# One load of x in place of two, and the second piece of w1 held behind a memset: a gated MLP on one core

## The chip, the cores and the metric

The kernel runs on one core of a Trainium2 chip. The metric is device time in microseconds (us). All times below are of this one core. A run counts as fast or slow by its distance from the fastest run of the same kernel (over 1.5% is slow).

## The reference, cut to what matters

```python
gate = jnp.einsum("bsd,df->bsf", x, w1)     # x: 32 x 32 tokens of 512, w1 and w3: 512 x 1792
up   = jnp.einsum("bsd,df->bsf", x, w3)
out  = jnp.einsum("bsf,fd->bsd", silu(gate) * up, w2)   # w2: 1792 x 512, all bf16
```

There are 1024 tokens. The contraction over 512 is four tiles of 128, called dt 0 to dt 3. The columns of w1 and w3 are 14 tiles of 128.

## The kernel before

Only the start matters here. TensorE runs six matmuls on a constant as its warm-up (0.77 to 3.49 us in the trace), turns the first 256 tokens of x by matmuls against an identity, and then multiplies these 256 tokens with the first four column tiles of w1 and of w3. The weights come in two pieces, dt 0 to 1 and dt 2 to 3. The second 256 tokens come turned by a DMA transpose.

```python
load_x(nc.sync, 0, 1)                                  # 128 tokens, 128 KB, issued by SP
load_x(nc.scalar, 1, 2)                                # 128 tokens, 128 KB, issued by ScalarE
load_w(nc.sync, w1_sb, w1_v, 0, FK, 0, 2)              # w1, dt 0-1, 256 KB
nc.scalar.activation(table[:], one, SIGMOID)           # ScalarE's table load comes here, 1.28 us
load_w(nc.scalar, w1_sb, w1_v, 0, FK, 2, DT)           # w1, dt 2-3, 256 KB
load_w(nc.sync, w3_sb, w3_v, 0, FK, 0, 2)
load_w(nc.sync, w3_sb, w3_v, 0, FK, 2, DT)
nc.sync.dma_start_transpose(out=xT[:, :, HB:NB], in_=x_flat[HB:NB, :])
for c0, c1 in ((FK, 8), (8, FT)):
    load_w(nc.sync, w1_sb, w1_v, c0, c1)
    load_w(nc.sync, w3_sb, w3_v, c0, c1)
# ... cut: one more transpose, w2, warm-up, turning x on TensorE
for dt in range(DT):
    for fo in range(FK):
        project(gates[fo], w1_sb, fo, 0, HB, [dt])     # 16 matmuls of 256 columns, dt by dt
for dt in range(DT):
    for fo in range(FK):
        project(ups[fo], w3_sb, fo, 0, HB, [dt])
```

Of the kernel before, what the change touches and what calls it, by code (L numbers as in the profile page):

```python
# [10 lines left out]
def kernel(  # L11
# [8 lines left out]
    nc = tc.nc  # L20
    P = nc.NUM_PARTITIONS
# [32 lines left out]
    w1_sb = consts.tile([P, DT, F], bf16, name="w1_sb")  # L54
# [6 lines left out]
    def load_x(queue, t0, t1):  # L61
        queue.dma_start(out=x_sb[:, t0:t1, :], in_=x_view[:, t0:t1, :])  # L62

    def load_w(queue, w_sb, w_v, c0, c1, d0=0, d1=DT):
        f0, f1 = c0 * P, c1 * P
        queue.dma_start(out=w_sb[:, d0:d1, f0:f1], in_=w_v[:, d0:d1, f0:f1])
# [1 line left out]
    one = nc.const_aps.tensor(1.0, [P, 1], bf16)  # L68
    table = consts.tile([P, 1], fp32, name="table")

    load_x(nc.sync, 0, 1)
    load_x(nc.scalar, 1, 2)
    load_w(nc.sync, w1_sb, w1_v, 0, FK, 0, 2)
    nc.scalar.activation(table[:], one, SIGMOID)  # L74
    load_w(nc.scalar, w1_sb, w1_v, 0, FK, 2, DT)
# [142 lines left out]
```

## Time and profile before

| kernel before | value |
|---|---|
| median of its six runs beside the changed kernel | 82.45 us (82.25 to 83.01) |
| span of the profiled run | 80.6 us |
| TensorE busy | 75.9 us |
| first gate matmul | 5.07 us |

How to read the profile's lines: the chain of waits lists start, duration and the work that the end hung on; a line of the timeline is start, duration, engine, source line, operation, tile, count, and in brackets how long the engine was idle before and what ended that. SPq and ACTq are the queues on which SP and ScalarE issue transfers.

### The profile page before, as it was taken

Reading aid. Unit: us, or ns where it says so; the run is one execution under the profiler, and the core shown is the slowest. Engines: PE = TensorE matmul, PEld = TensorE weight load, DVE = VectorE, ACT = ScalarE, POOL = GpSimd, SP = SyncE. Lnnn points to the kernel's source line nnn. Section 1 sums busy time; section 2 is a strip of 40 time slices with the busy share of each in tenths; the row PEclk is TensorE's granted clock in tenths of the full one; section 3 lists DMA queues with packets and bytes.
Section 4 is the critical chain, followed back from the end, with each engine's and each line's share of the span. In section 5 each row is a group of like instructions: output and inputs, shape, how many; then the busy total and the mean of one; then the engine's idle time right before and its main releaser. Section 6 shows DMA issues by size and latency. Waiting matters only on the chain.

```text
span 80.6 us, 1063 instructions
## 1 busy us (share of the span) xinstructions
PE 75.9 (94%) x404; PEld 38.8 (48%) x410; DVE 39.4 (49%) x61; ACT 23.2 (29%) x39; POOL 0.7 (1%) x6
## 2 busy tenths in 40 slices
PE   6959999999999999999999999999999999999960
PEld 2348984444444444444444444444444444444850
DVE  0110189999888878878868878872000000000040
ACT  4430274223432223432223432220220220220200
POOL 3000000000000000000000000000000000000000
PEclk9999999999999999999999999999999999999999
DMA  1999999989910000000000000000101102001120
GB/s 24 271 365 273 350 370 370 295 185 355 355 47 0 0 0 0 0 0 0 8 4 0 0 0 0 0 4 0 38 27 65 41 24 73 34 31 65 36 78 17
DMA packets 9893, 7.67 MB, mean 95 GB/s; under 512 B 3744, under 2 KB 9888, under 8 KB 9888
## 3 DMA queue, kind: packets, MB, share of 16 engines
q1 hardware_dynamic: 9472, 7.21, 29.6%
q10 hardware_dynamic: 416, 0.39, 1.4%
q8 instruction: 3, 0.05, 0.3%
q14 instruction: 2, 0.02, 0.1%
HBM read 5.77 MB, written 1.05 MB: 85 GB/s over the span
## 4 chain that ended last, share of the span: by engine, by line
PE 90%; DMA 5%; issue 1%; SPq 0%; DVE 0%; DVEq 0%
PE gate_ps L123 30%; PE o_ps L171 30%; PE up_ps L123 30%; DMA w_sb<-in_w_dram 5%; SPq L62 0%; DVE o_sb L180 0%; DVEq L180 0%
## 5 line engine op out<-in xcount | busy, mean ns | idle before, releaser
L123 PEld LDWEIGHTS <-w_sb 128*128 128x128 bf16 x256 | 25.0, 98 | 24.2 <-DMA w_sb<-in_w_dram 1.1
L123 PE MATMUL gate_ps<-xT,w_sb 128*128 128x512 bf16 (+1 forms) x126 | 28.7, 352 | 1.0 <-DMA w_sb<-in_w_dram 0.9
L123 PE MATMUL up_ps<-xT,w_sb 128*128 128x512 bf16 (+1 forms) x126 | 28.7, 352 | 0.1
L133 ACT ACTIVATE sig<-gate_ps 128x512 f32<-128x512 f32 x28 | 16.7, 597 | 32.0 <-PE gate_ps L123 29.7
L171 PE MATMUL o_ps<-w_sb,hT 128*128 128x512 bf16 (+2 forms) x138 | 24.3, 336 | 0.1
L135 DVE TENSOR_TENSOR t<-gate_ps,sig 128x512 f32<-128x512 f32 x28 | 19.3, 689 | 9.5 <-ACT sig L133 9.5
L136 DVE TENSOR_TENSOR hT<-t,up_ps 128x512 bf16<-128x512 f32 x28 | 19.3, 688 | 3.3 <-PE gate_ps L123 0.5
L171 PEld LDWEIGHTS <-hT 128*128 128x128 bf16 x140 | 12.6, 98 | 12.0
L180 DVE CAST o_sb<-o_ps 128x128 bf16<-128x128 f32 (+1 forms) x3 | 1.0, 336 | 22.3 <-PE o_ps L171 22.3
L182 ACT CAST o_sb<-o_ps 128x512 bf16<-128x512 f32 x7 | 4.1, 586 | 17.9 <-PE o_ps L171 17.9
L94 PE MATMUL warm_ps<-const-bfloat16-1.0 128*128 128x512 bf16 x6 | 2.7, 626 | 0.8 <-PEq L202 0.8
L116 DVE CAST xT<-pT 128x128 bf16<-128x128 f32 (+1 forms) x2 | 0.7, 358 | 3.7 <-PE pT L106 3.7
L94 PEld LDWEIGHTS <-const-bfloat16-1.0 128*128 128x128 bf16 x6 | 0.7, 136 | 1.8 <-issue 1.8
L74 ACT ACT_TABLE_LOAD x1 | 1.3, 1283 | 1.2 <-PEq L202 1.2
L116 ACT CAST xT<-pT 128x128 bf16<-128x128 f32 (+1 forms) x2 | 0.9, 426 | 1.2 <-PE pT L106 1.2
L106 PEld LDWEIGHTS <-x_sb 128*128 128x128 bf16 x8 | 0.5, 101 | 0.9 <-DMA x_sb<-in_x_dram 0.8
L106 PE MATMUL pT<-ident,x_sb 128*128 128x128 bf16 x8 | 0.7, 230 | 0.0
masks.py:199 POOL TENSOR_SCALAR_AFFINE_SELECT ident<-ident 128x128 bf16<-128x128 bf16 x1 | 0.3, 294 | 0.1
masks.py:197 POOL MEMSET ident<- 128x128 bf16 x1 | 0.2, 205 | 0.3 <-POOLq L202 0.3
L74 ACT ACTIVATE table<-const-bfloat16-1.0 128x1 f32<-128x1 bf16 x1 | 0.2, 203 | 0.0
L202 POOL MEMSET const-bfloat16-1.0<- 128x1 bf16 x1 | 0.1, 103 | 0.0
L202 POOL MEMSET const-uint8-127<- 128x1 uint8 x1 | 0.1, 103 | 0.0
(2 smaller groups left out, 0.2 us busy)
## 6 DMA issues: line engine op xcount, KB each, us to landing
w_sb<-in_w_dram SPq DMA_DIRECT2D x2, 896.0 KB, 7.0
w_sb<-in_w_dram SPq DMA_DIRECT2D x2, 768.0 KB, 8.1
w_sb<-in_w_dram SPq DMA_DIRECT2D x2, 512.0 KB, 5.8
out_dram<-o_sb SPq DMA_DIRECT2D x7, 128.0 KB, 1.7
w_sb<-in_w_dram SPq DMA_DIRECT2D x3, 256.0 KB, 4.3
w_sb<-in_w_dram ACTq DMA_DIRECT2D x1, 256.0 KB, 4.0
x_sb<-in_x_dram ACTq DMA_DIRECT2D x1, 128.0 KB, 2.8
x_sb<-in_x_dram SPq DMA_DIRECT2D x1, 128.0 KB, 2.6
```

The lines of the kernel that those rows point to most:

```text
L74: nc.scalar.activation(table[:], one, SIGMOID)
L94: nc.tensor.matmul(warm_ps[:, 0:cols], lhsT=one.to_broadcast([P, P]), rhs=one.to_broadcast([P, cols]), start=True, stop=True,)
L106: nc.tensor.matmul(pT[:, i, j, :], lhsT=x_sb[:, nt, dt * P : (dt + 1) * P], rhs=ident[:], start=True, stop=True,)
L116: copy(xT[:, dts[0] : dts[-1] + 1, nts[0] * P : (nts[-1] + 1) * P], pT[:].rearrange("p d t c -> p d (t c)"),)
L123: nc.tensor.matmul(ps[:, c0 : c0 + n1 - n0], lhsT=w_sb[:, dt, fo * P : (fo + 1) * P], rhs=xT[:, dt, n0:n1], start=(dt == 0), stop=(dt == D ...
L133: nc.scalar.activation(sig[:], gate_ps[:], SIGMOID)
L135: nc.vector.tensor_mul(t[:], gate_ps[:], sig[:])
L136: nc.vector.tensor_mul(hT[:, fo, nb * NB : (nb + 1) * NB], t[:], up_ps[:])
L171: nc.tensor.matmul(o_ps[:], lhsT=hT[:, fo, nt * P : (nt + 1) * P], rhs=w2_sb[:, fo, c0 : c0 + DB], start=(fo == 0), stop=(fo == FT - 1),)
L180: nc.vector.tensor_copy(o_sb[:], o_ps[:])
L182: nc.scalar.copy(o_sb[:], o_ps[:])
L202: nc = _bacc.Bacc("TRN2", target_bir_lowering=False, num_devices=1)
```

## The change

The intent: x goes first, alone and as one load, w1's first piece right behind it on the same queue. ScalarE issues only w1's second piece, and a memset of a part of that piece's place on GpSimd holds it back for a moment, so that it doesn't take bandwidth from x.

```diff
-    load_x(nc.sync, 0, 1)
-    load_x(nc.scalar, 1, 2)
+    nc.gpsimd.memset(w1_sb[:, 2, 0 : 2 * P], 0.0)
+    load_x(nc.sync, 0, 2)
     load_w(nc.sync, w1_sb, w1_v, 0, FK, 0, 2)
     nc.scalar.activation(table[:], one, SIGMOID)
     load_w(nc.scalar, w1_sb, w1_v, 0, FK, 2, DT)
```

## The prediction

> **What bounds the kernel now.** I read four views in turn: the page, the chain that ended last, the start of the timeline, and the transfers split by queue in two stretches of the start.
>
> The page says which engine is the bound, and how little is left beside it.
>
> ```profile
> span 80.6 us, 1063 instructions
> PE 75.9 (94%) x404; PEld 38.8 (48%) x410; DVE 39.4 (49%) x61; ACT 23.2 (29%) x39; POOL 0.7 (1%) x6
> PE 90%; DMA 5%; issue 1%; SPq 0%; DVE 0%; DVEq 0%
> ```
>
> TensorE is busy for 94% of the span. The third line is the chain that ended last: 90% is matmul, and only 5% is a transfer. The chain in order of time tells which transfer.
>
> ```profile
> 0.74 0.39 SPq L62
> 1.13 0.07 issue
> 1.20 3.83 DMA w_sb<-in_w_dram
> 5.02 0.05 issue
> 5.07 1.92 PE gate_ps L123 x16
> 6.99 1.75 PE up_ps L123 x16
> 8.74 0.44 PE gate_ps L123 x4
> ```
>
> So the end is set by the first piece of w1, issued by SP at 1.20 and landed at 5.02 us. The first gate matmul starts at 5.07, and from there TensorE runs without a gap worth naming to the last output tile. Whatever moves 5.07 moves the end; what does not move it is worth nothing. The timeline shows what TensorE does before that.
>
> ```profile
> 0.77 2.72 PE L94 MATMUL warm_ps<-const-bfloat16-1.0 128*128 128x512 bf16 x6 [0.77 <-PEq L202]
> 1.01 0.29 POOL masks.py:199 TENSOR_SCALAR_AFFINE_SELECT ident<-ident 128x128 bf16<-128x128 bf16 x1
> 1.23 0.44 ACTq L66 DMA_DIRECT2D w_sb<-in_w_dram  x1
> 3.39 0.75 PE L106 MATMUL pT<-ident,x_sb 128*128 128x128 bf16 x8
> 3.84 0.92 ACT L116 CAST xT<-pT 128x128 bf16<-128x128 f32 x2 [1.17 <-PE pT L106]
> 5.07 1.92 PE L123 MATMUL gate_ps<-xT,w_sb 128*128 128x256 bf16 x16 [0.94 <-DMA w_sb<-in_w_dram]
> ```
>
> Warm-up matmuls fill TensorE to 3.49. The transposes of x end at 4.14, and TensorE then sits idle 0.94 us for w1. The two halves of x landed at 0.74 + 2.6 = 3.34 (SP) and 0.73 + 2.8 = 3.53 (ScalarE), by the table of DMA issues. The ceiling of this change is the idle time, 0.94 us or 1.1% of 82.64: nothing ahead of 4.14 can be skipped, since the warm-up and the transposes lie there.
>
> [...] These are the transfers from 3.1 to 4.6 us, when the two pieces of w1 share the engines (q1 is SP's queue, q10 is ScalarE's: its 0.39 MB are x's second half and w1's second piece):
>
> ```profile
> DMA packets 538, 0.52 MB, mean 349 GB/s; under 512 B 27, under 2 KB 538, under 8 KB 538
> q1 hardware_dynamic: 278, 0.27, 52.7%
> q10 hardware_dynamic: 260, 0.26, 49.4%
> ```
>
> An even split, 278 to 260, of one total. From 4.6 to 5.1, when SP's queue is nearly alone (177 of 189 packets), the total is 373 GB/s: one queue fills the engines as well as two. And this is the start, from 1.5 to 3.1 us:
>
> ```profile
> DMA packets 315, 0.29 MB, mean 182 GB/s; under 512 B 31, under 2 KB 315, under 8 KB 315
> q1 hardware_dynamic: 171, 0.16, 52.7%
> q10 hardware_dynamic: 144, 0.13, 24.3%
> ```
>
> ScalarE's queue has moved 144 packets by 3.1: 128 of x and 16 small ones that count the completion. So w1's second piece has not begun by 3.1, though it was issued at 1.23[...]. That is a hold which the old kernel has for nothing, and the change gives it up.
>
> [...] The clock was up by about 3.5 us, so an earlier gate start would meet a fast TensorE. [...]
>
> **The change part by part.**
>
> (a) *One load of x on SP, 256 KB, in place of two of 128 KB.* SP's issue took 0.39 us for 128 rows; SP's three pieces of w1 and w3, of 256 rows of 1 KB each, took 1.43 in all, with the small gaps 0.48 each. So SP's later issues move back 0.05 to 0.08 us. [...] The first transpose now waits for all 256 tokens, not for 128; but the second needed the other half at 3.53 already.
>
> (b) *ScalarE's issue of x is gone.* Its queue is free at 0.73, its table load can start about 0.4 us sooner. It is idle before the copies at 3.84 in any case: worth nothing.
>
> (c) *The memset on GpSimd, 128x256 bf16.* A 128x1 memset took 103 ns, a 128x128 one 205, so 0.8 ns a column: an estimate of 103 + 255 x 0.8 = 0.31 us. It stands behind the identity's select, which ends at 1.30, so it ends at about 1.62 us. On TensorE's path it costs nothing.
>
> (d) *w1's second piece waits for it.* Issue goes from 1.23 to about 1.67. From SP's issue of x (0.74) to the first packets (the slices from 1.7 us on) it took about 1.0 us. With the same lag its packets would come from 2.67. In the old kernel they came after 3.1. So the hold makes up for most, not all, of the hold that is lost.
>
> (e) *When w1's first piece is through.* Count packets with the 16 that count each completion. SP's queue now holds x (256 + 16 = 272) and w1's first piece (272), together 544; ScalarE's holds 272. I take the old rates: 86 packets by 2.4 (64 and 22 on the two queues from 1.7 to 2.4), then 35 in 0.1 us (538 in 1.5 us is 36, 229 in 0.7 us is 33). By 2.67 SP's queue is at 86 + 2.7 x 33 = 175, with 369 to go. Split evenly, at 18 each, ScalarE's 272 take 1.51 us, to 4.18; SP has then done 272 more and has 97 left at 36, 0.27 us: 4.45. In the old kernel SP's queue needs 144 + 272 = 416 packets for the same piece. It had 171 + 278 = 449 by 4.6, so passed 416 near 4.5 to 4.55, and the landing was counted at 5.02, 0.5 later. With the same tail the new landing is 4.92 to 4.97. That is 0.05 to 0.1 us sooner, and it comes only from the slow stretch about 3.1 us (the page's 271 GB/s from 2 to 4), where the old kernel passes from x to w1 on both queues at once.
> Should the second piece start slowly, as it did in the old kernel (260 packets by 4.6, but hardly any before 3.3), the first gets more than half for 0.3 to 0.4 us. That is some 60 packets, or 0.15 us more.
>
> Sum: the gate starts 0.05 to 0.35 us sooner, and I take 0.2.
>
> (f) *What follows must keep up.* w1's second piece is needed 8 matmuls after the start (0.86 us); it landed at 1.23 + 4.0 = 5.23 and should now land about 5.0, against a need at 4.87 + 0.86 = 5.7. w3's pieces (landed near 5.95 and 6.78 by their issues and delays) are needed at 4.87 + 1.92 = 6.8 and about 7.7. The transposed half of the tokens, landed at 2.67 + 5.1 = 7.8, is needed near 8.4. All hold with 0.6 us or so to spare, so the gain passes to the end whole.
>
> 82.64 - 0.2 = 82.44; I say 82.45 us.
>
> **The rivals.**
>
> 1. *The hold is too short and the order is worse.* If w1's second piece meets x's own last packets at 2.67, x finishes later: 272 - 175 = 97 packets at 18 per 0.1 us reach 3.2, landing near 3.65 in place of 3.53. The first copies move from 4.11 to about 4.3, still ahead of w1. So x does not become the bound; the time stays at 82.5 to 82.7. For it: the count in (d). Against: the slow start of the second piece in the old trace.
>
> 2. *The hold works fully.* [...] At 36 per 0.1 us x's 272 are through by 2.9, and 70 packets of w1 by 3.1; the other 200 at 18 take 1.1 us, 4.2, landing 4.7. Gain 0.35 us, 82.3. For it: GpSimd's spans are rough, and a memset that takes 0.6 us would do it.
>
> 3. *SP's piece of w1 waits for the memset as well*, if the dependence were kept for the whole of w1's place. It would be issued at 1.67 in place of 1.25[...]. Cost 0 to 0.3 us. Against: two loads into disjoint parts of that place are already issued in parallel.
>
> 4. *TensorE turns cold or the transposes starve.* Warm-up matmuls run to 3.49 whatever x does, and the gap after the transposes only shrinks. I see no loss here.
>
> **Range and chances.** The steps give a gate start between 4.65 and 5.1, so -0.4 to +0.05 us. The three runs of the old kernel lie 0.6 us apart (82.41 to 83.01), as much as the effect, so I widen to 82.0 to 82.9. Faster by over 2% needs 1.65 us, more than the 0.94 us of idle time: 1%. Slower by over 2% would need the first gate matmul at 6.7 us, a load nobody foresees: 1%. Within 2%: 98%.
>
> **What would show it.** The chain should still run from a transfer of w1 to the first gate matmul, at 4.65 to 5.05; the idle time before the gate should be 0.4 to 0.9. GpSimd should show a 128x256 memset of 0.3 us from 1.3, and ScalarE's queue its issue near 1.7. ScalarE's first packets should be seen from 2.6 to 2.7; x should land at 3.3 to 3.65. From the gate start to the end, the duration should be unchanged (80.6 - 5.07 = 75.5 us). I am wrong if the chain goes through x's copies, or through w1's second piece; if TensorE waits again between the first gate and the transposed tokens; or if the memset takes over 1 us, so that the second piece becomes the late one.

## The result, and the profile after

The changed kernel took 88.02 us in the median (87.31 to 89.39, six runs), the kernel before 82.45 (82.25 to 83.01). The ratio is 1.0637, with a 95% interval of 1.058 to 1.070. Ratios here are the mean time of one kernel's fast runs over that of the other's fast runs of the same rounds, so not quite the ratio of the medians. The prediction of 82.45, within 82.0 to 82.9, was wrong by 5.6 us.

The profiled run of the changed kernel is one of the two that count as slow (89.39 us). Its parts are therefore compared below with another run, short_hold, which has the same wait with a shorter memset and was profiled in a fast run. These are the lines of the changed kernel's page, whose third line is the clock in 40 slices of 2.19 us, in tenths of full speed, and whose fourth and fifth are the chain by engine and by line:

```profile
span 87.6 us, 1065 instructions
PE 79.1 (90%) x404; PEld 40.4 (46%) x410; DVE 39.4 (45%) x61; ACT 23.2 (26%) x39; POOL 1.0 (1%) x7
PEclk9999555999999999999999999999999999999998
PE 85%; DMA 11%; issue 1%; DVE 0%; DVEq 0%; ACTq 0%
PE up_ps L123 29%; PE gate_ps L123 28%; PE o_ps L171 28%; DMA w_sb<-in_w_dram 8%; DMA x_sb<-in_x_dram 3%; DVE o_sb L180 0%; DVEq L180 0%; ACTq L66 0%
```

TensorE does the same 404 matmuls in 3.2 us more, three slices run at half clock, and the transfers' share of the chain has gone from 5 to 11%. A new name stands in the chain: ScalarE's queue at line 66. The start of the chain in order of time says what it does there:

```profile
0.74 2.78 DMA x_sb<-in_x_dram
3.51 0.02 issue
3.53 0.02 ACTq L66
3.55 0.04 issue
3.59 6.69 DMA w_sb<-in_w_dram
10.28 0.14 issue
10.42 1.87 PE gate_ps L123 x8
12.28 3.35 PE up_ps L123 x16
```

And these are lines from the start of the timeline:

```profile
1.24 0.31 POOL L71 MEMSET w_sb<- 128x256 bf16 x1
3.59 0.42 ACTq L66 DMA_DIRECT2D w_sb<-in_w_dram  x1
4.38 1.44 PE L123 MATMUL gate_ps<-xT,w_sb 128*128 128x256 bf16 x8
10.42 1.87 PE L123 MATMUL gate_ps<-xT,w_sb 128*128 128x256 bf16 x8 [4.59 <-DMA w_sb<-in_w_dram]
```

The memset is done at 1.55 us (1.62 was predicted). But ScalarE issues its piece of w1 at 3.59, two microseconds after that, right when x has landed (0.74 + 2.78 = 3.52). The piece lands at 10.28. The first eight gate matmuls, which need only the first piece, start at 4.38 and so 0.69 us earlier than before; then TensorE sits idle for 4.59 us, and what follows runs slowly.

The 7.0 us between the two profiled spans (87.6 and 80.6) divide as follows. In the kernel before the sixteen gate matmuls start at 5.07, the ninth of them (the first that needs w1's second piece) at 5.95; the ups end at 8.74. In the changed kernel the second eight start at 10.42: 4.47 us later. From there to the end of the ups it is 5.22 us (10.42 to 15.64) against 2.79 (5.95 to 8.74): 2.43 us. The rest, 71.96 against 71.86 us, is the same. Sum: 4.47 + 2.43 + 0.10 = 7.00.

The second part is the clock. The columns of the next lines are: stretch, its length, TensorE's busy time with its count, the same for its weight loads, granted clock, share of the DMA engines, GB/s; only work of line 123 is counted.

```profile
5.90:8.70 2.80, 0.00 (x0) 0.00 (x0) 0.99 1.11 128
8.70:10.40 1.70, 0.00 (x0) 0.01 (x1) 0.50 1.11 325
10.40:12.30 1.90, 1.88 (x10) 1.35 (x11) 0.50 1.10 351
12.30:15.60 3.30, 3.30 (x18) 2.38 (x17) 0.52 1.06 371
15.60:20.00 4.40, 4.35 (x37) 3.51 (x36) 1.00 1.07 274
```

TensorE stops at 5.82 us. The packed trace dates the changes of its clock: it falls to half at 8.62 and comes back at 15.45, long after work has begun again. In the kernel before the clock of these stretches was 1.00 throughout.

Two things about this record help in reading every run below. First, the changes lie 3.41 us or a multiple of it apart: 3.41 and 6.83 here, 3.41 and 3.41 in short_hold (9.14 and 12.55). So a stretch at half clock lasted one such step or two. One step at half costs 3.41 x 0.5 of some 86 us, or 0.02, in the mean clock; of the six runs of the changed kernel four have a mean of 0.98 (as short_hold's profile with its one step) and two have 0.958 (as this one with its two), so which it is differs between runs of one kernel. Second, the mean clock counts as 1.00 all that lies before the first recorded change. In the changed kernel that is at 5.21, and until then matmuls of 256 columns start 0.21 us apart, against 0.11 us after it: the first eight gate matmuls began at half clock. That cost nothing here, because TensorE had to wait afterwards. In the kernel before the record begins at 3.62, before the gate.

### The profile page after: what moved, and what is told of

It is laid out like the page before. It is cut to its first block, busy times and chain, and to the rows that moved or that the text cites. A ratio compares the mean times of both kernels' runs of the same rounds, so it can differ in the third digit from the quotient of the medians.

```text
span 87.6 us, 1065 instructions
## 1 busy us (share of the span) xinstructions
PE 79.1 (90%) x404; PEld 40.4 (46%) x410; DVE 39.4 (45%) x61; ACT 23.2 (26%) x39; POOL 1.0 (1%) x7
## 4 chain that ended last, share of the span: by engine, by line
PE 85%; DMA 11%; issue 1%; DVE 0%; DVEq 0%; ACTq 0%
PE up_ps L123 29%; PE gate_ps L123 28%; PE o_ps L171 28%; DMA w_sb<-in_w_dram 8%; DMA x_sb<-in_x_dram 3%; DVE o_sb L180 0%; DVEq L180 0%; ACTq L66 0%
## 5 line engine op out<-in xcount | busy, mean ns | idle before, releaser
L123 PEld LDWEIGHTS <-w_sb 128*128 128x128 bf16 x256 | 26.4, 104 | 29.4 <-issue 4.8
L123 PE MATMUL gate_ps<-xT,w_sb 128*128 128x512 bf16 (+1 forms) x126 | 30.1, 365 | 4.7 <-DMA w_sb<-in_w_dram 4.6
L123 PE MATMUL up_ps<-xT,w_sb 128*128 128x512 bf16 (+1 forms) x126 | 30.3, 370 | 0.1
```

The lines of the kernel that those rows point to most:

```text
L123: nc.tensor.matmul(ps[:, c0 : c0 + n1 - n0], lhsT=w_sb[:, dt, fo * P : (fo + 1) * P], rhs=xT[:, dt, n0:n1], start=(dt == 0), stop=(dt == D ...
```

## The experiments

**Why the piece waits for x.** The built program has the answer in the list of what each transfer waits for. This is ScalarE's transfer in the changed kernel, and below it the same transfer before (shortened; in a rebuild of both programs the waits are the same, with the one for DMAHW0 in an instruction just before the transfer):

```
after:   DMACopy w1_sb<-in_w1_dram 128x2x512 [waits DMAHW0, Pool]
before:  DMACopy w1_sb<-in_w1_dram 128x2x512
```

In these two programs the loads count their completion on eight semaphores, DMAHW0 to DMAHW7 in the list and eight numbers in the trace (102 to 109 in the changed kernel; 100, 102 and 104 to 109 before). The list takes them in turn over both issuing engines, in an order that is not that of the source. In the kernel before ScalarE's piece is among the first eight. With the memset in front of it, it comes behind all loads of SP that wait for nothing, and so is ninth. The ninth takes DMAHW0 again, whose first user is x, and waits until x's count is complete. The trace shows this wait: x and ScalarE's piece both count on number 102, and ScalarE's wait for 102 ends at 3.53, when x's sixteenth and last count has come at 3.51. Before, the piece counts on 106, which no earlier load has, and is issued at 1.23. No run leaves the wait out, so whether it is needed is not shown; the memset's cost lay in the ninth place that it led to. Theory A: the loss comes from this wait. Its main rival, B: the single load of x, or the new division of the queues, costs the time by itself.

The hold is first taken away altogether (no_hold):

```diff
-    nc.gpsimd.memset(w1_sb[:, 2, 0 : 2 * P], 0.0)
     load_x(nc.sync, 0, 2)
```

> The changed kernel without the memset, so ScalarE's piece of w1 waits for nothing and has a completion semaphore of its own. Theory A (the whole loss comes from that piece being issued at 3.59 us because its semaphore is the one that x's load uses, and the wait for it is for x's landing): ScalarE issues at 0.73, the first gate matmul starts near 5.1 and the time is 82.0 to 83.0 us. Rival B (one load of x, or the new split of the queues, is itself what costs): the time stays above 85 us.

Measured: 82.80 us in its one fast run, 84.37 in the median of four (82.80 to 85.07), against 82.7 of the kernel before. So most of the 5.6 us is gone, as A says. But in the profiled run, one of the slow ones, A's number for the gate was too early. ScalarE issued at 0.79 and its piece then shared the engines with x, so that x landed at 4.76; the first transposes of x began at 4.81, after 1.3 us of idle TensorE, and the first gate matmul at 5.94. Besides, its clock came up only at 9.55 (the listed mean of 1.0 hides that, as said above): the sixteen gate matmuls took 3.60 us in place of 1.92, which would explain 1.7 of the 2.3 us by which this run is above the fast one. Whether some hold is needed once ScalarE has no x of its own to issue stays open, since the fast run took no longer than the kernel before. There is no clean ratio from one fast run.

Next, the memset stays but is made short, or the semaphore is made free. In short_hold the memset is one column. In free_sem the two later loads of w1 are one, which puts ScalarE's piece among the first eight and gives it a semaphore of its own (the seventh, DMAHW6, in a rebuild; the expectation below calls it the eighth); the built program shows that it then waits for GpSimd alone.

```diff
# short_hold
-    nc.gpsimd.memset(w1_sb[:, 2, 0 : 2 * P], 0.0)
+    nc.gpsimd.memset(w1_sb[:, 2, 0:1], 0.0)
# free_sem (the memset as in the change)
+    load_w(nc.sync, w1_sb, w1_v, FK, FT)
     for c0, c1 in ((FK, 8), (8, FT)):
-        load_w(nc.sync, w1_sb, w1_v, c0, c1)
         load_w(nc.sync, w3_sb, w3_v, c0, c1)
```

> The changed kernel with the memset cut from 256 columns to one, so that GpSimd is done at 1.35 us and not at 1.55. In the built program ScalarE's piece of w1 is still the ninth load and still waits for the semaphore of x's load. Theory A (the hold is the wait for x's semaphore, the memset only moved the piece to ninth place): ScalarE issues near 3.55 us again, time 87.3 to 89.3 us. Rival M (the length of the memset sets the hold): issue near 1.4 us, time below 84.5 us.

> The changed kernel with its memset, but the two later loads of w1 are one, so that ScalarE's piece is the eighth load in the builder's order and not the ninth and waits for the memset alone. Theory A: ScalarE issues near 1.65 us, first gate matmul at 4.6 to 4.95, no later idle time, 82.0 to 82.5 us; this is the kernel that the prediction described. Rival C (any hold of that piece by GpSimd, even a short one, puts it behind the DMA transpose and makes it land at 8 us or later): 86 us or more.

short_hold: 87.61 us, ratio 1.061 (1.055 to 1.067). The memset's length does nothing. This is its timeline; the profiled run is a fast one:

```profile
1.24 0.10 POOL L71 MEMSET w_sb<- 128x1 bf16 x1
3.78 0.43 ACTq L66 DMA_DIRECT2D w_sb<-in_w_dram  x1
9.51 1.87 PE L123 MATMUL gate_ps<-xT,w_sb 128*128 128x256 bf16 x8 [3.33 <-DMA w_sb<-in_w_dram]
```

GpSimd is done at 1.34, ScalarE still issues only when x has landed (3.70 in this run). So what the slow profile of the changed kernel shows holds in the fast too. Here the parts are 3.56 us for the later start (9.51 against 5.95) and 1.46 for the clock (4.25 against 2.79 from there to the end of the ups, by its chain); the spans differ by 5.1 (85.7 against 80.6). The clock costs less than in the changed kernel's profile because it was at half for one step and not for two.

free_sem: 83.82 us, ratio 1.0129 (1.0085 to 1.0173). With the semaphore alone made free, four fifths of the loss are gone: 1.3% in place of 6.4%. That confirms A as the main cause; that the merged load of w1 does not do it by itself is shown by data_hold below, which has it too and is slow. But this was the kernel that the prediction described, expected at 82.0 to 82.5, and it is slower than the kernel before, clear of the noise though under 2%. Its timeline:

```profile
1.58 0.50 ACTq L66 DMA_DIRECT2D w_sb<-in_w_dram  x1
4.35 1.16 PE L123 MATMUL gate_ps<-xT,w_sb 128*128 128x256 bf16 x8
7.16 1.03 PE L123 MATMUL gate_ps<-xT,w_sb 128*128 128x256 bf16 x8 [1.64 <-DMA w_sb<-in_w_dram]
```

ScalarE issues at 1.58 and the first half starts at 4.35, both as hoped for. But the second piece lands at 1.58 + 5.44 = 7.02 (the duration is from its chain), not near 5. The second eight matmuls start at 7.16, which is 1.2 us later than the 5.95 of the kernel before, and that is the whole loss (83.82 - 82.7 = 1.1; the profiled spans differ by 1.3). The clock is at full speed from 4.60 on here. More on this below.

To rule out B from the other side, two_x_hold adds the memset alone to the kernel before:

```diff
+    nc.gpsimd.memset(w1_sb[:, 2, 0 : 2 * P], 0.0)
     load_x(nc.sync, 0, 1)
     load_x(nc.scalar, 1, 2)
```

> The kernel before with the memset alone added; x stays in two loads. Theory A: the memset puts ScalarE's piece of w1 tenth in the builder's order, it shares the semaphore of x's second half and is issued when that has landed, near 3.6 us; time 86.5 to 89 us. Rival B (the single load of x is what costs): 82 to 83 us.

Measured: 88.84 us, ratio 1.0726 (1.066 to 1.079). The record classes it as unclear, but its three fast runs, 88.10 to 89.13, all lie far above the kernel before. The memset alone makes the loss, with x still in two loads. In the built program the piece waits for DMAHW1, the semaphore of SP's half of x and not of ScalarE's, as was expected; so in the (slow) profile it was issued at 3.23, after that half had landed at 3.15, and not near 3.6.

**Is it the sharing or the lateness?** data_hold has a semaphore of its own for the piece, as free_sem, but GpSimd copies a bit of x into its place, which holds it by data until x has landed:

```diff
-    nc.gpsimd.memset(w1_sb[:, 2, 0 : 2 * P], 0.0)
     load_x(nc.sync, 0, 2)
+    nc.gpsimd.tensor_copy(w1_sb[:, 2, 0:P], x_sb[:, 0, 0:P])
```

> As the one before, with its semaphore of its own, but in place of the memset GpSimd copies 128x128 of x into the place of the piece, so the piece is held until x has landed, by data and not by a shared semaphore. Theory A in its narrow form (lateness is what costs, not the sharing as such): issue near 3.9, landing near 10 us, time 87 to 89 us. Rival D (a shared semaphore slows the transfer or its counting): issue near 3.9 but landing by about 6.5 us, time below 84.5 us.

Measured: 89.19 us, ratio 1.0686 (1.062 to 1.075); issue at 3.95, landing at 3.95 + 5.81 = 9.76. So the shared semaphore slows nothing by itself. The wait is what costs, whoever makes it.

**Why an issue two microseconds later lands five microseconds later.** The piece was issued at 1.23 and landed at 5.23 before; in the changed kernel it was issued at 3.59 and landed at 10.28. My first theory, T, was that its packets met those of the DMA transpose, which SP issues at 2.76. Two runs test it. plain_half puts a plain load of the same bytes in the place of the transpose, and late_turn moves the transpose behind the next load of w1:

```diff
# plain_half
-    nc.sync.dma_start_transpose(out=xT[:, :, HB:NB], in_=x_flat[HB:NB, :])
+    nc.sync.dma_start(out=xT[:, :, HB:NB], in_=x_flat[HB:NB, :].rearrange("(p t) (h c) -> p (t h) c", p=P, c=HB))
# late_turn
-    nc.sync.dma_start_transpose(out=xT[:, :, HB:NB], in_=x_flat[HB:NB, :])
     load_w(nc.sync, w1_sb, w1_v, FK, 8)
+    nc.sync.dma_start_transpose(out=xT[:, :, HB:NB], in_=x_flat[HB:NB, :])
```

> The changed kernel with the first DMA transpose (256 tokens) replaced by a plain load of the same 256 KB into the same place; the result is wrong on purpose. The late issue of ScalarE's piece near 3.6 us stays. Theory T (the piece is slow because its packets share the engines with those of the DMA transpose): it lands by 6.0 to 7.0 us and not at 10.3, the time falls to 83 to 84.5 us. Rival S (a piece issued that late is slow whatever SP's queue carries, since all loads issued before it on SP are ahead): it still lands after 8.5 us, 86 us or more.

> The changed kernel with the first DMA transpose moved behind the load of w1's second group of four column tiles; nothing is taken away and the result is right. Theory T: ScalarE's piece now meets plain loads, lands at 6.0 to 7.0 us, the first gate matmuls of its half follow then; the transposed tokens come later and may cost up to 1.5 us; time 83 to 85.5 us. Rival S: as the changed kernel, 87 to 89 us.

Both went against T. plain_half took 88.59 us (ratio 1.072; classed as unclear, with all four runs between 88.01 and 89.30), with the piece landing at 3.72 + 6.29 = 10.01; late_turn took 90.57 (1.0938), slower still and above both of its expectations, with the piece landing at 12.04. T falls as the cause. What the traces have in common is where the first packet of ScalarE's queue (q10) stands. In plain_half, from 1.5 to 7.1 us, so for 3.4 us after ScalarE's issue at 3.72:

```profile
DMA packets 1610, 1.35 MB, mean 241 GB/s; under 512 B 75, under 2 KB 1610, under 8 KB 1610
q1 hardware_dynamic: 1610, 1.35, 83.0%
```

Only SP's queue (q1) appears. It has moved 1.35 MB. The loads that SP had issued before ScalarE's 3.72 were x, one piece of w1, two of w3 and the plain load: five of 256 KB, or 1.31 MB, and a sixth was begun at 3.45. The same count in other runs: free_sem's first q10 packet came at 3.57, after some 0.48 MB; two loads (0.52 MB) had been issued before it. short_hold's came at 7.38; by 7.3 SP's queue had moved 1.28 MB, and five transfers, 1.31 MB, had been begun. This is theory F, the rival of plain_half's text made exact: loads on the two queues are served in the order in which they were issued, as if they stood in one line. In the changed kernel ScalarE issued in the middle of SP's 1.30 us of issuing the transpose (from 2.76); its packets began at 5.46, behind the four loads, and then ran among those of the transpose. F is rough where two issues overlap. short_hold's piece, issued in the same way during the transpose's issue, came behind nearly all of the transpose; no_hold's, issued 0.05 us after x, began when 0.12 of x's 0.26 MB had moved. It is also a little off in late_turn, where the piece began after 1.42 of the 1.57 MB of the five loads ahead of it.

The rival to F is now called S (not the S of plain_half's text): a late issue is late for some other reason, whatever SP has issued. sp_held decides, with one profile. It is data_hold with SP's fourth load, and so all that follows on SP, held in the same way:

```diff
     nc.gpsimd.tensor_copy(w1_sb[:, 2, 0:P], x_sb[:, 0, 0:P])
+    nc.gpsimd.tensor_copy(w3_sb[:, 2, 0:P], x_sb[:, 0, 0:P])
```

> As the run in which GpSimd copied x into the place of the piece (issue at 3.95, first packet at 7.36, landing at 9.76 us, 88.3 us), but SP's fourth load (w3's second piece) and all behind it are held in the same way by a second copy of x, so that SP has issued only x, w1's first and w3's first piece when ScalarE issues. Theory F (packets are served in the order in which loads were issued, whichever of the two queues they are on): the first packets come near 4.6 to 5.1 us, after w3's first piece, and the landing is at 6.2 to 7.0 us; the time falls to 83.5 to 86 us, w3 and the transposed tokens being later. Rival S (a piece issued near 4 us is late whatever SP has issued): first packets after 6 us, landing after 8.5, 87 us or more.

ScalarE issued at 4.09. The transfers from 1.5 to 5.1 us, and from 5.1 to 6.2:

```profile
DMA packets 808, 0.78 MB, mean 217 GB/s; under 512 B 45, under 2 KB 808, under 8 KB 808
q1 hardware_dynamic: 808, 0.78, 77.4%
```

```profile
DMA packets 137, 0.14 MB, mean 124 GB/s; under 512 B 4, under 2 KB 137, under 8 KB 137
q10 hardware_dynamic: 126, 0.13, 55.0%
q1 hardware_dynamic: 11, 0.01, 3.7%
```

Up to 5.1 SP's queue moves 0.78 MB, which is the three loads issued before ScalarE's (0.79 MB); then ScalarE's queue has the engines nearly to itself, though SP's next load was issued at 4.32. The first packet came at 5.16, where data_hold had it at 7.36. F holds for the order; S's "after 6 us" is out. The landing, however, was 4.09 + 4.21 = 8.30 and not 6.2 to 7.0, and the two fast runs took 86.26 and 86.74 us, between what F (83.5 to 86) and S (87 or more) had said. (These two runs give 86.50 to 82.52 or 1.048.) F was right about when the piece starts and says nothing of how fast it then runs. The stretch ran at 124 GB/s, a third of the 373 that SP's queue reached nearly alone in the kernel before. That second point stays open (see below).

**What the clock costs.** warm_wait puts 14 unread matmuls between the two halves of the gate, so that TensorE doesn't stop long:

```diff
     for dt in range(DT):
+        if dt == 2:
+            for _ in range(14):
+                nc.tensor.matmul(idle_ps[:], lhsT=one.to_broadcast([P, P]), rhs=one.to_broadcast([P, NB]), start=True, stop=True)
```

> The changed kernel with 14 matmuls of 512 columns that nobody reads, between the first and the second half of the first gate matmuls, so that TensorE is not idle for 4.6 us there. In the profile of the changed kernel the 24 matmuls after that gap took 5.22 us, against 2.6 in the kernel before. Theory A with the clock (of the 5.6 us lost, 1.5 to 2.6 are the slow clock after the gap): 85.0 to 86.5 us. Rival: the clock costs nothing extra, 87.5 to 88.5 us.

Measured: 86.62 us, ratio 1.0478 (1.043 to 1.053), against 1.0637 of the changed kernel. The clock in its three fast runs was 0.998 to 1.0, so no fall to half is recorded in them between the halves. (In the profiled run, the slow one of 88.90 us, it did fall, at 10.53, 2.0 us after the last of the 14.) The difference of the ratios, 0.016, is 1.3 us of 82.5, give or take 0.65 by the two intervals, near the 1.46 that short_hold's trace gives. So in fast runs the late piece costs some 4 us by its lateness and 1.3 to 1.5 by the clock.

**Can the idea be had without the wait?** all_sp issues all of it on SP, in the wanted order, with no memset. interleave starts from the kernel before and cuts w1's first 512 KB into four loads of one dt each, in turns on SP and ScalarE, so that dt 0 and 1 are through earlier:

```diff
# all_sp
-    nc.gpsimd.memset(w1_sb[:, 2, 0 : 2 * P], 0.0)
-    load_w(nc.scalar, w1_sb, w1_v, 0, FK, 2, DT)
+    load_w(nc.sync, w1_sb, w1_v, 0, FK, 2, DT)
# interleave (from the kernel before)
-    load_w(nc.sync, w1_sb, w1_v, 0, FK, 0, 2)
-    load_w(nc.scalar, w1_sb, w1_v, 0, FK, 2, DT)
+    load_w(nc.sync, w1_sb, w1_v, 0, FK, 0, 1)
+    load_w(nc.scalar, w1_sb, w1_v, 0, FK, 1, 2)
+    load_w(nc.sync, w1_sb, w1_v, 0, FK, 2, 3)
+    load_w(nc.scalar, w1_sb, w1_v, 0, FK, 3, DT)
```

> x in one load, and both pieces of w1 on SP[...], no memset, ScalarE issues nothing. If the order of the transfers is what counts, the first piece of w1 lands near 4.35 us as it did in the changed kernel, the second near 5.1, and the first gate matmul starts near 4.4 us: 81.6 to 82.2 us, below the kernel before. Rival: SP's later issues, 0.5 us later each, make the DMA transpose of the second half of the tokens the last to land: 82.3 to 83 us.

> The kernel before, without memset and with x in two loads, but w1's first 512 KB are in four loads of 128 KB, one per contraction tile, taken in turns by SP and ScalarE. If order of issue is what counts, the first two are through after 512 KB in all and not after 768: they land near 4.3 us, the gate starts at 4.3 to 4.5, the last two land near 5.1, and the time is 81.7 to 82.3 us, up to 0.7 us below the kernel before. Rival: as in the run with both pieces on SP, the engines drift apart after 3.7 us and a later piece lands after 6 us: 82.3 to 83.3 us.

Neither wins, and both miss the gain that was expected: all_sp 82.81 us, ratio 1.0027 (0.998 to 1.007); interleave 82.76, ratio 1.0003 (0.995 to 1.006). In interleave, as its rival said, a piece of the second half landed late, at 1.67 + 4.54 = 6.21. It also fell into the trap: with eight loads in place of six before it, SP's transpose is the ninth, waits for the semaphore of ScalarE's half of x and is issued at 3.80, not 2.67. In all_sp the first eight gate matmuls start at 4.49, 0.58 us earlier than in the kernel before, and the second eight at 6.53, 0.58 us later (5.95 before):

```profile
4.49 1.04 PE L122 MATMUL gate_ps<-xT,w_sb 128*128 128x256 bf16 x8
6.53 1.05 PE L122 MATMUL gate_ps<-xT,w_sb 128*128 128x256 bf16 x8 [1.01 <-DMA w_sb<-in_w_dram]
```

TensorE needs both halves before it can go on, so an earlier first half is worth nothing when the second is late. And the second is late while the engines slow down in between. Here are four stretches of 0.6 us, all_sp first, then the kernel before; the last two columns are the share of the DMA engines and GB/s:

```profile
3.00:3.60 0.60, 0.49 (x2) 0.00 (x0) 0.00 (x0) 0.00 (x0) 0.00 (x0) 1.00 1.04 362
3.60:4.20 0.60, 0.51 (x6) 0.52 (x7) 0.19 (x1) 0.08 (x1) 0.00 (x0) 1.00 0.94 277
4.20:4.80 0.60, 0.60 (x8) 0.58 (x7) 0.53 (x2) 0.29 (x2) 0.00 (x0) 1.00 0.82 179
4.80:5.40 0.60, 0.60 (x7) 0.40 (x5) 0.00 (x0) 0.47 (x1) 0.00 (x0) 1.00 0.83 244
```

```profile
3.00:3.60 0.60, 0.60 (x4) 0.15 (x3) 0.00 (x0) 0.00 (x0) 0.00 (x0) 1.00 0.90 280
3.60:4.20 0.60, 0.54 (x8) 0.36 (x7) 0.48 (x2) 0.29 (x2) 0.00 (x0) 1.00 1.06 369
4.20:4.80 0.60, 0.00 (x0) 0.00 (x0) 0.18 (x1) 0.56 (x1) 0.00 (x0) 1.00 1.10 382
4.80:5.40 0.60, 0.33 (x3) 0.31 (x4) 0.00 (x0) 0.00 (x0) 0.00 (x0) 1.00 1.07 360
```

From 4.2 to 4.8 all_sp moves 179 GB/s, the kernel before 382. In the trace of all_sp the sixteen completion counts of w1's second piece arrive between 4.76 and 6.49 us: the last comes 1.7 us after the first (below called the drift of the engines). In the kernel before those of the same piece arrive between 4.80 and 5.27.

**What stays open.** Why the engines drift apart. It came with w3's third-placed piece (the changed kernel: counts from 4.69 to 6.37), with w1's (all_sp: 4.76 to 6.49), so it isn't one tensor. Where only the rate or the landing is known, these look the same: with a plain load in the transpose's place the rate fell as well (plain_half: 80 GB/s at 4.2 us); it fell with one queue at work (all_sp: 179 GB/s from 4.2 to 4.8) and with two (free_sem: 164, its piece landing at 7.02); and a piece landed late with x in one load and in two (interleave: 6.21). The kernel before, which has both pieces of w1 in flight side by side, lacks it at this place (4.80 to 5.27, 382 GB/s). No run takes its cause away by itself.

## Why the prediction was wrong

- **What bounds the kernel** was right for the kernel before: w1 sets the first gate matmuls, and from the end of the ups on nothing moved (71.96 against 71.86 us in the two spans). "Whatever moves 5.07 moves the end" was too strong: all_sp moved it to 4.49 and won nothing, and the changed kernel moved it to 4.38 and lost, since the second half of the gate then set the end.
- **(a), (b), (c)** held. x landed at 3.51 (3.3 to 3.65 was said), the memset took 0.313 us from 1.24, and ScalarE's earlier table load was worth nothing.
- **(d) failed, and with it the prediction.** It said that the piece waits for the memset, "Issue goes from 1.23 to about 1.67." Measured: 3.59, because the memset had made the piece the ninth transfer on eight semaphores and so made it wait for x. The trace before could not show that the ninth place was taken. A look at the order of the built program would have; I read the diff only as an edge between GpSimd and ScalarE. Rival 3 came near (a further dependence), but put it on SP's piece, as a matter of overlapping places.
- (d) also took "the same lag" of 1.0 us from issue to first packet. Measured: 2.0 us in free_sem and 1.87 in the changed kernel, with SP's loads ahead, as F has it. That the old kernel's piece came after x's second half (issued at 1.23, 8 of its packets begun by 3.3) is true as far as it goes; F is the wider form.
- **(e)** had the right direction and too small a size. It said 4.92 to 4.97 for w1's first piece from an even split with the second. With the second piece behind it there is no split: the first gate matmuls started at 4.38 in the changed kernel, 4.35 in free_sem. Its sum was off as well: it has SP's 416th packet in the kernel before at 4.5 to 4.55, where the packed trace has it at 4.41. The tail to 5.02 is then 0.61 us, and with it the even split would have given 5.06, no gain.
- **(f) failed.** "w1's second piece ... should now land about 5.0". It landed at 10.28 in the changed kernel, and at 7.02 even in free_sem, where (d) holds. This is what kept the intended kernel from its gain.
- **Rival 4** said that no cold clock was to be feared, as "the gap after the transposes only shrinks". It did, but a new gap of 4.59 us opened between the halves of the gate, and half clock cost 1.3 to 2.4 us. Nor did the earlier gate "meet a fast TensorE": the clock came up at 5.21 in the changed kernel's profile and at 4.60 in free_sem's, after the gate's start. The profiled kernels all run the same six warm-up matmuls at the same times, and their recorded clocks came up anywhere from 3.62 (the kernel before, near the prediction's "about 3.5 us") to 9.55 (no_hold), so these matmuls alone did not fix when the clock came up.
- The list of what would prove it wrong named the case: "if the chain goes through ... w1's second piece". The 1% given to a loss over 2% was far too little for a change that adds an edge between engines to the start of a kernel.

## What to carry to other kernels

A new dependence can cost more than the work behind it (here 5.6 us for a memset of 0.31): before predicting, look in the built program for what each transfer now waits for, completion semaphores included, and count whether it still has one of its own. In these runs an early load that was issued late didn't lose only the delay, it went behind what had been issued in the meantime (changed kernel: issued 2.36 us later than before, landed 5.05 us later); so to hold a load for a moment, think of holding the loads behind it as well. (sp_held did so: its piece began 2.2 us sooner than data_hold's and its fast runs were some 1.8 us faster, but still slower than the kernel before.) A piece that lands earlier helps only if the piece needed right after it doesn't land later (all_sp: first half 0.58 us earlier, second 0.58 us later, ratio 1.0027).

## What the traces show besides

- In the kernel before, loads issued side by side (1.20 and 1.23) shared the engines nearly evenly (278 to 260 packets from 3.1 to 4.6 us). In the changed kernel and the runs built on it, a load on ScalarE's queue issued later than SP's loads got almost no packet before theirs were through, apart from the overlaps named under F: in sp_held SP's queue moved its 0.78 MB of three loads by 5.1 us before ScalarE's, issued at 4.09, began at 5.16.
- From the start of an issue to the first packet it took 1.0 us with nothing ahead (SP's x in the kernel before, issued from 0.74 to 1.13, first packet at 1.76), which is 0.63 us from the end of the issue; with loads ahead it was 2.0 (free_sem) to 3.4 us (plain_half) from the start.
- One load on SP's queue counted its completion over 1.7 us (4.76 to 6.49 in all_sp), with the rate down to 179 GB/s.
- 13 of the DMA transpose's 256-byte packets in the changed kernel, begun from 5.8 to 6.7 us, took 0.26 to 1.10 us and all ended at 6.90 to 6.94, as if they waited for the last one. This is read from the packets' times; no run tested it.
- The recorded changes of the clock lie 3.41 us or a multiple of it apart. The clock fell after steps of 3.41 us that held 0.6 us of matmuls (the changed kernel, 5.21 to 8.62) and 1.4 us (warm_wait, 7.12 to 10.53), and stayed up over one that held 1.65 us (data_hold, 3.63 to 7.05). It was down 2.8 us after the last matmul in the first case and 2.0 in the second.
- On GpSimd a memset of bf16 on 128 partitions took 0.103 us for one column, 0.205 for 128 and 0.313 for 256.
